# Head of batch 0 by feature halves, and new step plans, in a fused attention and token/channel mixing kernel

## The chip, the cores and the metric

One core of a Trainium2 chip. The metric is the device time of one execution in microseconds (us), the median of several runs. A ratio is the mean time of one kernel's runs over that of the other's runs in the same rounds, so it is not quite the ratio of the medians quoted beside it. Profiles cover one execution each; their span is about 1.8 us shorter than the time. The granted clock is the share of TensorE's full clock that the profile records as granted.

The engines: TensorE (PE, with its weight loads PEld), VectorE (DVE), ScalarE (ACT), GpSimd (POOL), SyncE (SP).

## The reference

Pooled attention with 8 batches, 8 heads, 576 tokens and head size 64, followed by a mixer: keys and values are averaged over groups of 8 tokens, so each head has 72 keys. The result is rearranged to x (576 tokens by 512 features) and goes through token mixing and channel mixing.

```python
k_p = k.reshape(B, H, 72, 8, D).mean(axis=3)            # and v_p
attn = softmax(q @ k_p.T / sqrt(D));  x = attn @ v_p     # -> (B, S, H*D)
h = np.maximum(xt @ w_tok1, 0.0) @ w_tok2                # token mixing, xt = x transposed
u = x + h.transpose(0, 2, 1)
out = u + np.maximum(u @ w_ch1, 0.0) @ w_ch2             # channel mixing, 512 -> 1536 -> 512
```

## The kernel before

Batch 0 has a *head* of its own: a list of steps that runs before any channel mixing can start. Then follow nine *units* (eight batches, and one for the 64 last tokens of all batches). A unit is 48 half-steps of channel mixing on PE: in the first 24 w_ch1 products (a group of four 512-column matmuls per two half-steps, ScalarE applies the relu), in the last 24 w_ch2 products. A *plan* says after which half-step which step of the attention of the next batches is put in: a bare name is for the next batch, `>` for the one after, `<` for the same one. The program gives each engine its instructions in the order in which the steps are put in, so a plan fixes the order on each engine.

```python
HEAD = """c0 c1 d8 q0 d1 q1 d5 kp0 kp1 kt0 d2 o0 e0 kt1 kp2 kp3 o1 e1 kt2 kt3 q2 q3 d2 o2 e2 vpool0 o3 d1 vpool1 e3 d2
          av1 av0 av2 d2 av3 at_0 at_2 av4 at_1 at_3 d2 at_4 X0 X1 X2 A0 A1 A2 X3 A3 d3"""
FIRST = {0: "<u0 lv2", 1: "<u1", 2: "<u2", 3: "<u3", 4: "k0 kpool1 lk3", 5: "Q0 Q1 Q2 Q3", 10: "kpT v0 v1 lq3 lv3",
         13: "s0", 17: "s1", 22: "s2", 24: "av0", ...}
FOURTH = {0: ">K0 >K1 >V0 >V1 at0", 1: "at1", 3: "u4 M4", 4: "u0", 6: "u1 M0", 7: "u2", 9: "u3 M2 M",
          15: ">Q0", 17: ">Q1", 18: ">kpT", 22: ">s0", 26: "T0", 27: ">Q2 >Q3 lq4 lk4 lv4", ... 32: ">s1", ...
          37: ">s2", 39: ">av0", 41: ">av1", 43: ">av2", 45: ">av3", 47: ">av4"}
```

(cut; SECOND, THIRD and LATER are alike.) The steps: `q`, `Q` q transposes by PE and by DVE; `k`, `v`, `kp`, `kpool`, `vpool`, `K`, `V` pooling; `kt`, `kpT` key transposes; `o`, `e`, `s` scores with exp on ScalarE; `av` attention times values, normalised by DVE; `at` first token product with relu; `u` second token product plus x, an add by DVE; `t` u transposed by PE; `M`, `T` the same by a round trip through memory and DVE block transposes; `X`, `A` the parts of u transposed directly in the head; `dN` N dummy matmuls that keep PE busy; `l` loads.

The pools hold eight PSUM banks (128 x 512 fp32 each): three accumulators of one bank (`p1`), two of two banks (`p2`), one more (`pt`).

```python
ps_one = ctx.enter_context(tc.tile_pool(name="ps_one", bufs=3, ...))   # p1
ps_two = ctx.enter_context(tc.tile_pool(name="ps_two", bufs=2, ...))   # p2
ps_tr  = ctx.enter_context(tc.tile_pool(name="ps_tr",  bufs=1, ...))   # pt
def u(c):                                   # cut: c < 4
    ps = ps_one.tile([P, 512], FP32, name="p1")
    for i, (w, a) in enumerate(mms):
        nc.tensor.matmul(out=ps, lhsT=w, rhs=a, start=(i == 0), stop=(i == len(mms) - 1))
    nc.vector.tensor_tensor(out=dst, in0=ps, in1=x, op=ALU.add)
```

The softmax here doesn't subtract the row's maximum and nothing guards it: scores larger than these inputs give would overflow.

## Time and profile before

| | before |
|---|---|
| time, median of the five runs beside the changed kernel | 280.1 us (279.3 to 280.5) |
| span of the profile | 278.3 us |
| PE busy | 268.9 us, 97% |
| first channel matmul | 24.75 us |
| last matmul ends | 274.5 us |
| waits of PE in the list, after 24.7 us | 1.3 us |

The 1.3 us are these five groups (what waited, for what, "issue" being nothing that the profile shows; us in total, times, longest). The prediction below shows the other lines and splits the time by them.

```profile
PE p L445 <- issue: 0.3, 2, 0.2
PE p L467 <- issue: 0.3, 2, 0.2
PE p L225 <- DMA kr<-in_k_dram: 0.3, 1, 0.3
PE p L297 <- ACT ex L263: 0.2, 1, 0.2
PE p L343 <- DVE xt L315: 0.2, 1, 0.2
```

### The profile page before, as it was taken

The page shows a single profiled execution, that of the slowest core. Times are in us where ns is not written, and L with a number is a line of the kernel's source. Part 1 is how long each engine was busy: PE and PEld are TensorE (multiplying, and loading weights), DVE is VectorE, ACT ScalarE, POOL GpSimd, SP SyncE. Part 2 cuts the span into 40 slices and gives each one's busy share as a digit, 9 for nine tenths or more (in the row PEclk, how much of TensorE's full clock was granted, in tenths as well). Part 3 has the DMA queues.
Part 4 walks back from the last instruction along what each step waited for, and adds up shares of the span by engine and source line. Part 5 has one row for each costly group of instructions (what it writes and reads, how often), then busy time and mean ns, then how long its engine had stood idle before and what let it go on. Part 6 is the DMA issues. An engine that isn't in the chain of part 4 may idle for free.

```text
span 278.3 us, 4495 instructions
## 1 busy us (share of the span) xinstructions
PE 268.9 (97%) x1790; PEld 130.9 (47%) x1824; DVE 141.8 (51%) x272; ACT 111.2 (40%) x187; POOL 130.8 (47%) x121
## 2 busy tenths in 40 slices
PE   8989999999999999999999999999999999999994
PEld 3755445444543545454445444544454444444443
DVE  5465967771575757275178545834584161011012
ACT  2543590039305533614741366046604602602600
POOL 8585222999996992898069999600000000000000
PEclk9999999999999999999999999999999999999999
DMA  7999999980299930793549562324132545015024
GB/s 162 185 203 206 205 203 187 225 179 10 24 180 180 231 50 0 138 218 89 115 74 241 144 129 49 77 66 126 38 78 57 136 71 115 0 39 113 2 44 108
DMA packets 36837, 32.68 MB, mean 117 GB/s; under 512 B 14288, under 2 KB 30288, under 8 KB 36816
## 3 DMA queue, kind: packets, MB, share of 16 engines
q0 software_dynamic: 18672, 17.64, 40.2%
q1 hardware_dynamic: 17984, 14.62, 20.9%
q8 instruction: 14, 0.23, 0.3%
q10 hardware_dynamic: 160, 0.13, 0.2%
q14 instruction: 7, 0.06, 0.1%
HBM read 38.21 MB, written 11.80 MB: 180 GB/s over the span
## 4 chain that ended last, share of the span: by engine, by line
PE 83%; DMA 8%; ACT 3%; DVE 2%; POOL 2%; issue 1%; POOLq 0%
PE p L467 32%; PE p L445 30%; PE p L358 6%; PE p L343 5%; DMA kr<-in_k_dram 5%; PE p L258 4%; PE p L297 3%; DMA f<-in_moe_w_tok_dram 3%; ACT ex L263 1%; PE pt L368 1%; PE p L479 1%; ACT GT L449 1%; DVE o L453 1%; POOL vr L86 1%; POOL kr L86 1%
## 5 line engine op out<-in xcount | busy, mean ns | idle before, releaser
L467 PE MATMUL p<-w_ch,GT 128*128 128x512 bf16 x404 | 99.2, 379 | 1.0 <-issue 0.3
L449 ACT ACTIVATE GT<-p 128x512 bf16<-128x512 f32 x108 | 64.0, 599 | 75.8 <-PE p L445 75.6
L445 PE MATMUL p<-uT,w_ch 128*128 128x512 bf16 x373 | 92.7, 379 | 1.1 <-issue 0.3
L445 PEld LDWEIGHTS <-w_ch 128*128 128x128 bf16 x432 | 40.3, 98 | 48.1 <-issue 4.9
L467 PEld LDWEIGHTS <-GT 128*128 128x128 bf16 x420 | 38.0, 98 | 41.9 <-issue 3.1
L453 DVE TENSOR_TENSOR o<-p,u 128x512 f32<-128x512 f32 x32 | 21.9, 684 | 31.4 <-PE p L467 31.2
L263 ACT ACTIVATE ex<-p 72x1024 bf16<-72x1024 f32 (+1 forms) x42 | 31.6, 807 | 10.8 <-PE p L258 10.8
L146 POOL TENSOR_TENSOR t<-t 72x512 f32<-72x512 f32 x24 | 30.3, 1262 | 1.9
L145 POOL TENSOR_TENSOR t<-kr 72x1024 f32<-72x1024 bf16 x12 | 25.5, 2123 | 8.5 <-DMA kr<-in_k_dram 7.8
L359 DVE TENSOR_TENSOR u<-p,x 128x512 bf16<-128x512 f32 x32 | 22.1, 691 | 13.9 <-PE p L358 13.6
L145 POOL TENSOR_TENSOR t<-vr 72x1024 f32<-72x1024 bf16 x12 | 25.4, 2120 | 0.9
L390 DVE STREAM_TRANSPOSE uT<-v 128x512 bf16<-128x512 bf16 x16 | 10.4, 686 | 23.7 <-DMA v<-mem 23.7
L334 ACT ACTIVATE AT<-p 128x512 bf16<-128x512 f32 x8 | 4.8, 597 | 42.0 <-PE p L343 39.2
L315 DVE TENSOR_TENSOR x<-p,den 128x512 bf16<-128x512 f32 x30 | 20.7, 691 | 1.0
L246 DVE STREAM_TRANSPOSE qD<-qb 128x576 bf16<-128x576 bf16 x28 | 20.5, 794 | 0.0
L297 PEld LDWEIGHTS <-ex 72*128 72x128 bf16 x320 | 15.3, 98 | 10.4 <-DVE x L315 0.8
L358 PE MATMUL p<-AT,w_tok 128*128 128x512 bf16 x63 | 18.8, 379 | 0.0
L297 PE MATMUL p<-vp,ex 72*128 72x65 bf16 x320 | 16.8, 194 | 1.0 <-DVE x L315 0.6
L309 DVE RECIPROCAL den<-p 128x8 f32<-128x8 f32 (+1 forms) x39 | 7.9, 203 | 17.5 <-PE p L297 16.6
L103 POOL DMA_DIRECT2D qb<-in_q_dram x7 | 5.1, 730 | 21.5 <-DVE qD L246 20.3
L343 PE MATMUL p<-x,w_tok 128*128 128x512 bf16 x54 | 14.1, 379 | 0.1
L336 DVE TENSOR_SCALAR AT<-p 128x512 bf16<-128x512 f32 x8 | 5.5, 692 | 13.4 <-PE p L343 12.6
(90 smaller groups left out, 206.4 us busy)
## 6 DMA issues: line engine op xcount, KB each, us to landing
out_dram<-o SPq DMA_DIRECT2D x70, 128.0 KB, 2.5
kr<-in_k_dram POOLq DMA_DIRECT2D x7, 576.0 KB, 11.8
qb<-in_q_dram POOLq DMA_DIRECT2D x7, 576.0 KB, 11.1
vr<-in_v_dram POOLq DMA_DIRECT2D x7, 576.0 KB, 15.2
w_ch<-in_moe_w_ch_dram POOLq DMA_DIRECT2D x6, 512.0 KB, 13.2
mem<-u SPq DMA_DIRECT2D x8, 256.0 KB, 2.1
v<-mem SPq DMA_DIRECT2D x8, 160.0 KB, 3.8
v<-mem SPq DMA_DIRECT2D x8, 128.0 KB, 3.0
```

The lines of the kernel that those rows point to most:

```text
L145: eng.tensor_tensor(out=t4[:, 0:n], in0=t[:, hs, 0:4], in1=t[:, hs, 4:8], op=ALU.add)
L146: eng.tensor_tensor(out=t4[:, 0:n, 0:2], in0=t4[:, 0:n, 0:2], in1=t4[:, 0:n, 2:4], op=ALU.add)
L263: nc.scalar.activation(out=exv[:, a, :, gs.start:gs.stop, n0:n0 + n], in_=pss[a][0:SP, :, 0:len(gs) * n].rearrange("j l (g n) -> j l g n", ...
L297: nc.tensor.matmul(out=halves[h // 4][:, (h % 4) * (D + 1):(h % 4 + 1) * (D + 1)], lhsT=st["ex"][:, h * S + n0:h * S + n0 + P], rhs=st["vp ...
L315: nc.vector.tensor_tensor(out=dst.rearrange("p (a h d) -> p a h d", a=2, d=D), in0=view[:, :, :, 0:D], in1=den[rows, :, :, None].broadcast ...
L343: nc.tensor.matmul(out=ps, lhsT=w_tok1[:, c if c < 4 else 4 + par, m * P:(m + 1) * P], rhs=st["x"][:, c, :] if c < 4 else st["xt"], start= ...
L358: nc.tensor.matmul(out=ps, lhsT=w, rhs=a, start=(i == 0), stop=(i == len(mms) - 1))
L359: nc.vector.tensor_tensor(out=dst, in0=ps, in1=x, op=ALU.add)
L445: nc.tensor.matmul(out=ps, lhsT=w_ch1[:, kk, m * P:(m + 1) * P], rhs=uT[:, kk, :], start=(kk == 0), stop=(kk == 3))
L449: nc.scalar.activation(out=GT[:, m, :], in_=ps, func=AF.Relu)
L453: nc.vector.tensor_tensor(out=o_sb, in0=ps, in1=(u_tails if n == B else st["u"])[:, c, :], op=ALU.add)
L467: nc.tensor.matmul(out=pss[c], lhsT=GT[:, m, c * P:(c + 1) * P], rhs=w_ch2[:, m, :], start=(m == 0), stop=(m == NM - 1))
```

## The change

Its intent: shorten the head, and place all steps with a model of the timeline. In the head, heads 4 to 7 are scored by token chunk instead of by pair; AV, normalising and token mixing are done per four heads, so that the first half can flow while the second is scored; u transposed is made in two passes; the later dummies are dropped. All plans are new, and the first unit takes the w_ch2 weights in fours (before: eight, then four).

```diff
+        def half_av(c, a, eng, bank):        # cut: four heads, one bank
+                for l in range(4):
+                    nc.tensor.matmul(out=ps[:, l * (D + 1):(l + 1) * (D + 1)], lhsT=st["ex"][...], rhs=st["vp"][:, h, :], ...)
+                nc.vector.reciprocal(out=den[rows], in_=view[:, :, D])
+                if eng == "D":  nc.vector.tensor_tensor(out=dst..., in0=view[:, :, 0:D], in1=den..., op=ALU.mult)
+                else:           # four scalar.activation(Copy, scale=den)
-        def at_tile(c):                      # two 512-column matmuls
+        def at_half(c, a, ms):               # 256 columns of one or both
+        def zscore(i):                       # heads 4 to 7, tokens of four, four and one blocks of 64
-            runs[0:2] = [(c, m, m + w) for m, w in ((0, 8), (8, 4)) for c in range(2)]
+            runs[0:2] = [(c, m, m + 4) for m in (0, 4, 8) for c in range(2)]
-    HEAD = (above)
+    HEAD = """c0 c1 d8 q0 d1 q1 d5 kp0 kp1 kt0 kp2 e0 o0 kt1 kp3 kt2 o1 q3 q2 e1 kt3 vpool0 z2 z0 w30A w10Dt
+              w00D z1 w20Dt vpool1 w40Dt g21 w11D w21Dp g20 g11 g40 g31 g10 w01D g30 g00 w31D h1 w41Dp g41 h0 h2
+              h3 g01 X1 h4 X2 Xa X3 Xb A0 A1"""
-    FIRST, SECOND, THIRD, FOURTH, LATER = (above)
+    FIRST = {0: "<u3 <u1", 1: "<u2 <u0", 2: "k0 lv2", 4: "Q0 Q1", 5: "lk3", 6: "lq3 Q3 Q2", 9: "v0", 10: "kpool1",
+             11: "lv3", 12: "kpT", 14: "s0", 15: "v1", 19: "s1", 25: "s2", 26: "av0", 27: "av1", 29: "av2", ...}
+    FOURTH = {0: "M4 u4 >K1", 1: "at0 at1 >K0", 3: "u0 >V0", 5: "u1 M0", 6: ">V1", 7: "u2", 8: "u3 M2", 9: "M",
+              15: ">kpT >Q1", 17: ">Q0", 22: "lq4", 25: ">Q2", 26: ">s0", 27: "T0", 28: ">Q3 lk4 lv4", ... 32: ">s1 T2", ...
+              39: ">av0", 41: ">av1", 42: ">av2", 45: ">av3", 46: ">av4"}
```

(cut: SECOND, THIRD, LATER, the other plan entries, the rewritten steps for u transposed, the registration of the step names, and two statements that are only written differently.)

## The prediction

> **What bounds the kernel now.** I read the page first, then busy time by stretch, then TensorE (PE) in order of time, because the change touches only the first 25 us and the order of steps after it.
>
> ```profile
> span 278.3 us, 4495 instructions
> PE 268.9 (97%) x1790; PEld 130.9 (47%) x1824; DVE 141.8 (51%) x272; ACT 111.2 (40%) x187; POOL 130.8 (47%) x121
> ...
> PE 83%; DMA 8%; ACT 3%; DVE 2%; POOL 2%; issue 1%; POOLq 0%
> ```
>
> PE is the bound. DVE, ACT and POOL are near half, so moving work onto them is free unless it lies in PE's way. The stretches tell where PE is not full:
>
> ```profile
> 0.00:5.00 5.00, 3.81 (x12) 1.56 (x13) 2.66 (x9) 1.96 (x2) 3.87 (x11) 1.00 0.63 158
> ...
> 24.70:52.00 27.30, 26.76 (x186) 12.71 (x188) 20.33 (x33) 12.36 (x22) 8.70 (x9) 1.00 1.26 198
> ...
> 246.00:274.50 28.50, 28.34 (x141) 13.88 (x142) 5.26 (x8) 7.17 (x12) 0.00 (x0) 1.00 0.28 62
> 274.50:278.30 3.80, 0.00 (x1) 0.00 (x0) 0.42 (x1) 0.00 (x0) 0.00 (x0) 1.00 0.42 98
> ```
>
> The second column is PE's busy time. From 24.7 to 274.5 us PE is busy nearly throughout, and the listed waits of PE after 24.7 us add up to 1.3 us, the longest 0.3. So time = (start of the first channel matmul) + (about 250 us of PE work) + 3.8 us of tail. The change does not touch the amount of work after the head. It can move the start, and it can remove or add small waits.
>
> ```profile
> 1.19 3.60 PE L513 MATMUL pt<-warm 128*128 128x512 bf16 x8 [1.19 <-DVE warm L535]
> ...
> 17.89 0.43 PE L297 MATMUL p<-vp,ex 72*128 72x65 bf16 x8 [0.55 <-DVE x L315]
> ...
> 20.96 0.59 PE L326 MATMUL p<-xt,w_tok 128*128 128x512 bf16 x2
> 21.39 0.83 PE L400 MATMUL p<-ident,x 128*128 128x128 bf16 x12
> 22.06 1.55 PE L408 MATMUL p<-w_tok,AT 128*128 128x512 bf16 x6
> 23.45 0.39 PE L400 MATMUL p<-ident,x 128*128 128x128 bf16 x4
> 23.89 0.38 PE L408 MATMUL p<-w_tok,AT 128*128 128x512 bf16 x1
> 24.10 0.81 PE L513 MATMUL pt<-warm 128*128 128x512 bf16 x3
> 24.75 0.59 PE L445 MATMUL p<-uT,w_ch 128*128 128x512 bf16 x2
> ```
>
> L513 are dummy matmuls. The head ends at 24.75 with three of them (24.10 to 24.75, 0.216 us each), right in front of the first channel matmul. Before that, the fourth mixing block is done late (23.45 and 23.89), after the other three.
>
> ```profile
> 17.74 0.17 DVE L303 RECIPROCAL den<-p 128x4 f32<-128x4 f32 x1
> 17.95 0.42 DVE L304 TENSOR_TENSOR x<-p,den 128x256 bf16<-128x256 f32 x1
> 18.29 0.17 DVE L303 RECIPROCAL den<-p 128x4 f32<-128x4 f32 x1
> 18.50 0.42 DVE L304 TENSOR_TENSOR x<-p,den 128x256 bf16<-128x256 f32 x1
> 18.84 0.20 DVE L309 RECIPROCAL den<-p 128x8 f32<-128x8 f32 x1
> ```
>
> VectorE sets the middle of the head: from 16.64 to 20.78 it normalises the AV results one after another. A half of a chunk (four heads) recurs every 0.55 us (17.74, 18.29, 18.84); a whole one takes 0.20 + 0.69 with small gaps, about 0.95. This is the price list for the change.
>
> **What the Trainium skill says.** "TensorE: Matmul & The Clock Gate", Back-to-back issue gap: N/2.4 + 2.5 ns, 216 ns at N = 512. The trace agrees (three dummies in 0.65 us). Same page, What's actually happening: the array runs at half rate until it has been busy for a window of about 3.4 us, and falls back after an idle one. The first eight dummies take 3.60 us, 0.45 each, so this trace shows the slow state once; the longest gap in the rest of the head is 0.55 us. "VectorE: DVE Perf Modes", The TRN2 errata: a fixed cost per instruction, so two halves cost more than a whole. The trace agrees: 0.42 us for 256 elements against 0.69 for 512.
>
> **The change part by part.**
>
> (a) Dummies. d8, d1, d5 stay; fourteen later ones go (2+2+1+2+2+2+3), 3.0 us of PE at 0.216. Most stood in waits and are worth nothing; the last three, 0.65 us, stood in front of the first channel matmul, though the last uT copy (ACT, 24.30 to 24.89) would have held part of that.
>
> (b) Heads 4 to 7 are scored by token chunk. Four exps (0.59 + 0.70 twice = 2.58 us of ACT) become two of 1024 columns and one of 256; in the first unit's score steps two exps of 72x1024 take 1.93 and two of 72x256 take 0.69, so 0.96 each and 0.35, together 2.3. ACT saves 0.3 us; the gain in order is that AV and mixing of heads 0 to 3 start before heads 4 to 7 are scored.
>
> (c) AV by halves. Ten halves: one by ACT (4 x 0.22 = 0.87), nine by DVE, 9 x 0.55 = 4.95 us. Before: DVE had four chunks, about 4.1 us. DVE gains 0.8 us of work, but may start some 2 us earlier.
>
> (d) Token mixing by halves: 20 matmuls of 256 columns instead of 10 of 512, the same 2.2 us of streaming. The last one before AT is now 2 x 0.11 instead of 2 x 0.22.
>
> (e) uT in two passes: all first-half products (4 x 0.216), then all second-half ones; the late fourth block disappears.
>
> My walk through the new head, with the landings and durations above. The loads are issued in the same order, so they land as before: the last v piece needed by the first value pooling is there at about 12.75 (the trace starts it at 12.95). Value pooling 12.75 to 13.8, its copy on DVE 13.8 to 14.25. z2, z0 on PE to 14.3; ACT exps z2 to 14.3, z0 to 15.3, first half chunk on ACT to 16.2, z1 to 17.1. DVE: reciprocal at 14.65, half chunks 14.85, 15.4, 15.95, then 0.2 us of waiting for the second value pooling, its copy 16.7 to 17.1, then six half chunks at 0.55: 17.1 + 3.3 = 20.4. (Before: 20.78.) Last mixing matmuls 20.5 to 20.85, relu ACT 20.8 to 21.4, DVE 20.9 to 21.6 (before 21.98 and 22.28). The 12 transposing matmuls left fit in the relu's shadow. A0 21.45 to 22.3, A1 22.3 to 23.2. Copies: DVE 22.7 to 23.4, ACT 22.95 to 23.55, DVE to 24.1, ACT to 24.1. The first channel matmul needs the first copy: **23.5 us instead of 24.75, 1.25 us earlier.**
>
> (f) First unit. Before, PE waited 0.27 us at 29.23 for the key load of batch 1, issued at 15.59 and 13.60 us on its way:
>
> ```profile
> 15.59 13.60 DMA kr<-in_k_dram
> 29.23 1.06 PE p L225 x8
> ```
>
> That pooling moves from step 4 to step 10. PE gets there at 23.5 + 8 x 0.216 (u) + 22 x 0.216 + waits of (g) = 30.4, after 29.2: 0.27 us gained. The key transpose follows at 32.1 (DVE's half, 29.2 + 2.4 = 31.6, is ready), the scores at 33.15, where the two q transposes end at 33.0. That is tight: it is the supply that would stop a still faster head.
>
> (g) The u products now come two by two in steps 0 and 2. There are three one-bank accumulators and each u needs a DVE add of 0.69 before its bank is free: by the same walk waits of 0.1, 0.25 and 0.08, 0.43 us, against 0.16 before. Lost: 0.27.
>
> (h) The other plans. What is left to gain is what PE still waits for after the first unit: 0.9 us in listed waits (four of 0.2 or so) and about seven of 0.08 on u accumulators, some 1.4 us. A plan placed by a model of the timeline may take part of it and may make new ones. I take 0.3 us.
>
> Sum: 1.25 + 0.27 - 0.27 + 0.3 = 1.55 us; 280.0 - 1.6 = **278.4 us**.
>
> **The rivals.**
> 1. *VectorE sets the head.* It has 0.8 us more to do. If the halves cannot start until about 16 us (the accumulators or the exps come late), its chain ends at 21.5 or later and the start stays at 24.7. Against: values are ready at 14.25 and DVE has nothing else then. It would make the time 279.8.
> 2. *The clock.* Without dummies PE is thinner between 10 and 21 us, and a fall to half rate would double the streaming time of what follows until the next busy window: some 3 us, time 281 to 283. Against: no wait in the walk reaches 1 us, and the measured ones with dummies were 0.55 at most.
> 3. *The transfers.* DMA is saturated until about 55 us (share 1.26 in the stretch above). The w_ch2 pieces land near 36.8, 39.9 and 43.0; PE needs the first at 40.4 before, about 38.8 after, and the new order in fours asks the second at 41.4 and the third at 44. Margin 1 to 2 us. If it failed, the head's gain would be given back there: 279.5 to 280.
> 4. *The plans make waits.* Reordering 200 steps may turn some 0.2 us waits into more; up to 1 us either way.
>
> **Range and chances.** Rivals 1 and 3 give back at most the gain; rival 2 is unlikely. The best I can sum (head 1.8, plans 1.2) is 277.0. So 278.4, with 277.0 to 280.1 eight times in ten. Two per cent is 5.6 us; PE's idle time before 25 us (25 less 22.7 busy, 2.3), the removed dummies (3.0) and the waits after it (1.3) together are hardly more, and most of the head hangs on transfers. Faster by over 2%: 0.02; within: 0.97; slower: 0.01.
>
> **What would show it.** Right: the first channel matmul at 23 to 24 us, no wait of PE on the key load, DVE half chunks every 0.55 us from about 14.8 to 20.4 in the order of PE, PE's end moved by the same 1 to 2 us. Wrong: the first half chunks on DVE after 16 us; PE gaps over 1 us in the head, or matmuls of 512 columns spaced 0.43 us; a wait on w_ch or on qD between 33 and 45 us; a list of PE waits after 60 us that sums to over 1.5 us.

## The result

275.5 us (274.9 to 276.0, five runs) against 280.1 in the same rounds: ratio 0.984, 95% interval 0.982 to 0.986. That is 4.6 us less, within 2% as predicted most likely, but outside the predicted range of 277.0 to 280.1.

The page of the changed kernel (span; busy time and instructions of each engine):

```profile
span 273.7 us, 4544 instructions
PE 266.1 (97%) x1832; PEld 130.4 (48%) x1832; DVE 141.9 (52%) x280; ACT 110.4 (40%) x182; POOL 131.1 (48%) x121
```

PE is the bound as before, and its share has not moved: 97%. A reader who looks only at this line sees nothing of where 4.6 us went. The order of time on PE, at the end of the head (start, duration, what):

```profile
21.28 1.92 PE L461 MATMUL p<-w_tok,AT 128*128 128x512 bf16 x8
23.34 0.59 PE L512 MATMUL p<-uT,w_ch 128*128 128x512 bf16 x2
...
30.22 1.04 PE L226 MATMUL p<-kr,ident 72*72 72x256 bf16 x8
```

The first channel matmul (L512) comes at 23.34, 1.41 us earlier than at 24.75; the walk had said 23.5. The key pooling at 30.22 has no wait any more (the walk: 30.4). PE's last matmul ends at 269.95 in the chain of the changed kernel and at 274.51 before. From first channel matmul to last that is 246.6 us against 249.8: **3.15 us less for exactly the same matmuls.** The predicted net gain for this part was 0.3 us.

So where were 3.15 us of waiting, if the list of PE's waits after 24.7 us added up to 1.3 in all (and to 0.4 in the changed kernel)? Two places of the kernel before, in order of time on PE:

```profile
128.86 0.59 PE L358 MATMUL p<-AT,w_tok 128*128 128x512 bf16 x2
129.38 0.81 PE L445 MATMUL p<-uT,w_ch 128*128 128x512 bf16 x3
...
150.86 0.81 PE L343 MATMUL p<-x,w_tok 128*128 128x512 bf16 x3
151.87 0.38 PE L343 MATMUL p<-xt,w_tok 128*128 128x512 bf16 x1 [0.20 <-DVE xt L315]
```

Look at the starts, not at the idle times. Two matmuls at 128.86 should let the next start 2 x 0.216 later, at 129.29; it starts at 129.38, 0.08 us late (a `u` accumulator whose add is not done), and no idle time is printed. Three at 150.86 should let the next start at 151.51; it starts at 151.87, 0.36 late, and 0.20 is printed. The record of a matmul of 512 columns lasts 0.379 us while matmuls follow each other every 0.216, so 0.163 us of every wait lies under the modelled end of the matmul before it. The Trainium skill says of these records ("Perfetto Trace Analysis", Per-instruction lifecycle) that TensorE's end is estimated, not observed; the trace puts the 0.163 on it. The same place in the changed kernel runs through, 4 x 0.216 from start to start:

```profile
146.93 1.03 PE L395 MATMUL p<-x,w_tok 128*128 128x512 bf16 x4
147.79 0.38 PE L395 MATMUL p<-xt,w_tok 128*128 128x512 bf16 x1
```

I then took, for every two neighbouring matmul records, the time from start to start less the streaming time of what the program has between them (N/2.4 + 2.3 ns at N columns, other small constants for the narrow ones; where a record is missing the next one is taken). The sums by unit, in us; the score steps have a fixed extra cost of about 0.36 a batch in it (three score steps, 0.12 each), the same in all kernels. Its level depends on the constants for the narrow matmuls; the differences between the kernels do not:

| kernel | first channel matmul | unit 0 | 1 | 2 | 3 | 4 | 5 | 6 | all |
|---|---|---|---|---|---|---|---|---|---|
| before | 24.75 | 1.56 | 2.41 | 1.02 | 0.73 | 0.89 | 0.53 | 0.18 | 7.4 |
| changed | 23.34 | 1.47 | 1.09 | 0.49 | 0.37 | 0.36 | 0.36 | 0.02 | 4.2 |

Take off 7 x 0.36 = 2.5 and 4.9 us could be had before, of which the list showed 1.3; 1.7 are left after. The gain is in units 1 to 6, which the old plans left 0.2 to 1.3 us a unit worse. For these six alone, the sums are 5.8 and 2.7 us, of which 6 x 0.36 = 2.2 are fixed: 3.6 us could be had, and the new plans took 3.1 of them. Units 7 and 8 have nothing beside them and no wait in either.

### The profile page after: what moved, and what is told of

Same layout as the page of the kernel before. It is cut to its first block, busy times and chain, and to the rows that moved or that the text cites. A ratio compares the mean times of both kernels' runs of the same rounds, so it can differ in the third digit from the quotient of the medians.

```text
span 273.7 us, 4544 instructions
## 1 busy us (share of the span) xinstructions
PE 266.1 (97%) x1832; PEld 130.4 (48%) x1832; DVE 141.9 (52%) x280; ACT 110.4 (40%) x182; POOL 131.1 (48%) x121
## 4 chain that ended last, share of the span: by engine, by line
PE 89%; DMA 3%; ACT 3%; DVE 2%; POOL 1%; issue 1%; POOLq 0%
PE p L534 33%; PE p L512 32%; PE p L410 6%; PE p L395 6%; PE p L344 3%; PE p L260 3%; DMA vr<-in_v_dram 3%; ACT ex L265 1%; PE pt L420 1%; ACT GT L516 1%; PE p L226 1%; PE p L546 1%; POOL kr L86 1%; PE pt L376 1%; PE p L461 0%
## 5 line engine op out<-in xcount | busy, mean ns | idle before, releaser
L534 PE MATMUL p<-w_ch,GT 128*128 128x512 bf16 x420 | 101.5, 379 | 0.0
L512 PE MATMUL p<-uT,w_ch 128*128 128x512 bf16 x384 | 92.8, 379 | 0.1
L512 PEld LDWEIGHTS <-w_ch 128*128 128x128 bf16 x432 | 40.6, 98 | 47.3 <-issue 2.5
L147 POOL TENSOR_TENSOR t<-t 72x512 f32<-72x512 f32 x24 | 30.4, 1265 | 1.9
L362 DVE TENSOR_TENSOR x<-p,den 128x512 bf16<-128x512 f32 x28 | 19.4, 692 | 1.0
L386 ACT ACTIVATE AT<-p 128x512 bf16<-128x512 f32 x7 | 4.2, 597 | 32.2 <-PE p L395 32.2
L344 PEld LDWEIGHTS <-ex 72*128 72x128 bf16 x280 | 13.0, 98 | 7.9 <-DVE x L362 0.7
L356 DVE RECIPROCAL den<-p 128x8 f32<-128x8 f32 (+1 forms) x35 | 7.1, 202 | 15.9 <-PE p L344 15.4
L344 PE MATMUL p<-vp,ex 72*128 72x65 bf16 x280 | 14.1, 193 | 0.2 <-ACT ex L265 0.2
L260 PE MATMUL p<-qD,kD 32*72 32x512 bf16 (+1 forms) x224 | 11.4, 294 | 0.1
```

The lines of the kernel that those rows point to most:

```text
L147: eng.tensor_tensor(out=t4[:, 0:n, 0:2], in0=t4[:, 0:n, 0:2], in1=t4[:, 0:n, 2:4], op=ALU.add)
L344: nc.tensor.matmul(out=halves[h // 4][:, (h % 4) * (D + 1):(h % 4 + 1) * (D + 1)], lhsT=st["ex"][:, h * S + n0:h * S + n0 + P], rhs=st["vp ...
L512: nc.tensor.matmul(out=ps, lhsT=w_ch1[:, kk, m * P:(m + 1) * P], rhs=uT[:, kk, :], start=(kk == 0), stop=(kk == 3))
L534: nc.tensor.matmul(out=pss[c], lhsT=GT[:, m, c * P:(c + 1) * P], rhs=w_ch2[:, m, :], start=(m == 0), stop=(m == NM - 1))
```

## The experiments

Theory P: the surprise is many short waits of PE that the plans removed. Theory H: the earlier head carries the rest along. Rivals of detail came up on the way.

**1. The new head with the old plans.** The changed kernel with `FIRST` to `LATER` and the order in eights put back.

> The new head with the old step plans and the old order in eights. Theory P (the plans carry the surprise): the first channel matmul comes at 23.3 us as in the changed kernel, but the old first plan has the key pooling of batch 1 at step 4; PE gets there near 27.6 and stands until the keys land near 29.1, a wait of about 1.5 us that takes the head's 1.4 us back. So 279.7 to 280.2 us. Theory H (the head carries it, the rest follows from an earlier start): 277 us or less.

Measured 280.89 us against 280.21 (ratio 1.002, 0.9996 to 1.0036): the head alone gains nothing. The start was at 23.38 as expected. Its longest listed waits after 24 us:

```profile
PE p L260 <- DVE qD L248: 1.0, 2, 0.7
PE p L226 <- DMA kr<-in_k_dram: 0.5, 1, 0.5
```

The wait on the keys (L226) was only 0.64 us from start to start (0.5 listed), since the keys landed near 28.4; that part of the expectation was too large. The u accumulators took 0.5. The rest went in unit 3, where the scores (L260) stood for the q transposes, and these stood on DVE behind the first block transpose, which waited for the round trip through memory: one store of u took 4.3 us to land instead of 2.1. Unit 3's sum was 1.99 instead of 0.73. So the total came near the expected one (0.7 above its range), but in part by two further waits that I had not foreseen.

**2. The new plans with the old head.** The kernel before with `FIRST` to `LATER` and the order in fours of the changed one.

> The old head with the new step plans and the order in fours. Theory P: first channel matmul at 24.75 as before, then the 3.1 us of small waits are gone, 276.8 to 277.4 us. Theory H: 279.5 us or more.

Measured 277.14 us (ratio 0.988, 0.986 to 0.990): theory P. In its trace the sum of small waits is 3.9. Its first channel matmul came at 25.38; seven profiled runs with the old head and its dummies spread from 24.75 to 25.67, so the profile of before was at the early end. This kernel and the changed one differ by the head alone: 277.14 and 275.5 us, 1.6 apart by the medians and some 1.2 by the two ratios (0.988 and 0.984).

**3. Only the plans of the second and later units.**

```diff
-    SECOND, THIRD, FOURTH, LATER = (old)
+    SECOND, THIRD, FOURTH, LATER = (new)      # FIRST, HEAD and the order in eights stay
```

> The kernel before with only the plans of the second and later units replaced. By start-to-start times of TensorE the first unit holds about 1.2 us of small waits in both kernels, so under theory P nearly all of the 3.1 us comes here: 276.9 to 277.6 us. If the new first plan carried it: 279 us or more.

Measured 277.41 us (ratio 0.9895, 0.988 to 0.991). Nearly all of the plans' gain is here, 0.3 us at most in the first unit.

**4. The complement: the changed kernel with the old later plans.**

```diff
-    SECOND, THIRD, FOURTH, LATER = (new)
+    SECOND, THIRD, FOURTH, LATER = (old)      # new HEAD, new FIRST
```

> The changed kernel with only the plans of the second and later units put back to the old ones. Theory P with the sums of small waits by unit: the old later plans hold 3.1 us more than the new ones, so 275.5 + 3.1 = 278.6 us, up to 279.9 if unit 3 meets the wait on the q transposes that the head-only run met (1.3 us). Theory H (the early start carries the rest with it): 276.5 or less.

Measured 279.97 us median (ratio 0.9985, 0.995 to 1.002), in two groups: 278.6, 278.9, 279.1 and 280.8, 280.9, 280.9. The lower group is at the expected 278.6, though not for the expected reasons alone: the profiled run, the one of 278.62 us, had 1.51 in unit 3 already (0.8 more than before), and its channel started at 22.85, 0.5 earlier than in the changed kernel's profile. What makes the upper group 2 us slower was not seen in a trace and stays open; the granted clock of two of its runs was 0.991 and 0.994, of the third 0.999. Theory H (276.5) falls.

**5. Three kinds of short waits taken out by hand.** The kernel before with three sets of moves: S for score steps, U for u products, X for the last AV chunks, which write the tail of x.

```diff
-  FIRST  ... 17: "s1", 22: "s2", 24: "av0"      +  18: "s1", 23: "s2", 25: "av0"       # S; alike in SECOND and THIRD
-  LATER  ... 4: "u0", 6: "u1 M0", 7: "u2", 9: "u3 M2 M"
+             5: "u0", 7: "u1 M0", 9: "u2", 11: "u3 M2 M"                                # U; FOURTH alike
-  FOURTH ... 43: ">av2", 45: ">av3", 47: ">av4" +  42: ">av2", 44: ">av3", 46: ">av4"  # X; in THIRD av3 and av4 alone
```

> The kernel before with three kinds of waits taken out by hand, none of which the list of waits shows in full: the second score step one step later in the first three units (0.27 us four times, the exps not done), the u products of the later units two steps apart (0.08 us eight times, the add not done), the fifth AV chunk one step earlier in the third and fourth unit (0.21 and 0.36 us, the tail of x not ready). Theory P in detail: 2.2 us together, 277.6 to 278.2 us. If these short waits were not real, or only moved, 279.5 us or more.

Measured 279.62 us (ratio 0.9966): 0.9 us instead of 2.2. In the trace the waits of U and X were gone (0.64 and 0.57 less). Those of S were gone at `s1` and partly back at `s2` (0.23 or 0.25, three times) and at an AV step (0.37, twice). In unit 3, where `M` now starts two half-steps later, some 0.5 came up in front of the scores, on the q transposes that stand behind the first block transpose. The next three runs take these apart.

**6. S alone.**

> The kernel before with only the second score step (and the third and the first AV with it) one step later in the first three units. From the run of all three edits: the four waits of 0.27 us go, but 0.23 us comes back at the third score step three times and 0.37 at the first AV twice, since ScalarE has 6.5 us of exps and relus to do in that stretch. So no gain: 279.7 to 280.3 us. If the distance of the steps were all: 279.0 us.

Measured 280.09 us (ratio 0.9992, 0.998 to 1.0005): no gain, as expected. ScalarE in the kernel before, in order of time:

```profile
61.49 1.93 ACT L263 ACTIVATE ex<-p 72x1024 bf16<-72x1024 f32 x2 [0.39 <-PE p L258]
63.31 1.07 ACT L449 ACTIVATE GT<-p 128x512 bf16<-128x512 f32 x2
64.26 1.94 ACT L263 ACTIVATE ex<-p 72x1024 bf16<-72x1024 f32 x2
66.07 1.58 ACT L449 ACTIVATE GT<-p 128x512 bf16<-128x512 f32 x3
67.50 0.69 ACT L263 ACTIVATE ex<-p 72x256 bf16<-72x256 f32 x2
```

From 61.49 to 68.19 it has no pause: exps (L263) and the channel relus (L449) share it. An engine that is busy 40% of the span is the bound for these 6.7 us, and a step moved by one half-step only changes which matmul waits for it.

**7. U and X with a well-meant third move.** The q transposes of unit 3 put before the first block transpose:

```diff
-  FOURTH ... 26: "T0", 27: ">Q2 >Q3 lq4 lk4 lv4"
+             25: ">Q2 >Q3", 26: "T0", 27: "lq4 lk4 lv4"     # and U with "u0 u1 M0" at 5, and X
```

> The kernel before with two of the three hand edits, the ones whose waits vanished in the run of all three: the u products of the later units where no accumulator is short (0.08 us eight times), the fifth AV chunk earlier (0.21 and 0.36), and in unit 3 the q transposes put before the first block transpose on VectorE, so that they cannot stand behind a transfer. The score steps stay. Theory P: 1.1 to 1.3 us less, 278.9 to 279.2 us. If short waits only move: 279.8 us or more.

Measured 283.13 us median, 280.7 to 288.5 (ratio 1.006): slower. Two of the six runs, 287.4 us and the profiled one, 288.5, count as slow by being over 1.5% above its fastest; the four fast ones (280.7 to 283.5) are slower than the kernel before too, but none of them was traced. The trace of the slow one shows a collision. DVE, then the transfers issued between 133 and 137 us (count, KB each, us to landing):

```profile
150.08 0.71 DVE L390 STREAM_TRANSPOSE uT<-v 128x512 bf16<-128x512 bf16 x1 [16.21 <-DMA v<-mem]
```

```profile
qb<-in_q_dram POOLq DMA_DIRECT2D x1, 576.0 KB, 5.7
kr<-in_k_dram POOLq DMA_DIRECT2D x1, 576.0 KB, 10.1
vr<-in_v_dram POOLq DMA_DIRECT2D x1, 576.0 KB, 14.3
v<-mem SPq DMA_DIRECT2D x4, 128.0 KB, 10.2
```

The q buffer came free 7 us earlier, so the loads of the next batch were issued at 134.2 us instead of 141.6, on top of the four reads of the round trip (v<-mem). Those landed up to 150 us instead of 139, DVE stood 16 us for them, PE stood twice (5.0 and 2.6 us), and the granted clock was 0.50 from 148.5 to 158.7 us.

**8. The same without that move.**

> The run with the u and AV edits again, but with the q transposes of unit 3 left behind the first block transpose as in the kernel before. In the earlier run the q buffer came free 7 us sooner, the next batch's loads were issued at 134 instead of 141 us and took the bandwidth from the round trip of u through memory (landed at 150 instead of 139). Theory L (that collision alone made it slow): this one is 1.0 to 1.3 us under the kernel before, 278.9 to 279.2, with the loads issued near 141 us. If the u and AV edits themselves cause it: 282 us or more again.

Measured 278.85 us (278.6 to 279.1, ratio 0.995, 0.994 to 0.996): 1.3 us less, theory L, and every run is below the fastest one with the third move. The reads of the round trip:

```profile
v<-mem SPq DMA_DIRECT2D x4, 128.0 KB, 3.5
```

They land in 3.5 us again. Twelve moved entries of the plans, and waits of which not one is listed above 0.2 us, are worth 1.3 us.

**9. The plans-only kernel without the fourteen later dummies.** This tests the rival of the clock.

> The kernel of the plans-only run without the fourteen later dummy matmuls of the old head. If the dummies cost only where they stand before ready work: the channel matmuls start 0.4 to 0.8 us earlier, 276.3 to 276.8 us. If the clock needs them, 512-column matmuls in the head are spaced 0.43 us and the time is 278 us or more. What is then left to the changed kernel's 275.5 is what the halves bring, 0.8 to 1.2 us.

Measured 277.27 us (276.2 to 277.7, ratio 0.988, 0.986 to 0.991) against 277.14 with the dummies in the earlier rounds: no gain, and between my two expectations. The stretches of the head in its trace (PE's busy time second, the granted clock third from the end), and two rows of PE:

```profile
18.00:20.00 2.00, 1.40 (x11) 0.57 (x12) 1.90 (x7) 1.35 (x7) 1.94 (x5) 0.78 1.25 206
20.00:22.00 2.00, 2.00 (x13) 1.03 (x12) 1.26 (x3) 0.00 (x0) 2.00 (x3) 0.50 1.24 206
```

```profile
18.88 1.83 PE L326 MATMUL p<-x,w_tok 128*128 128x512 bf16 x4
...
25.75 0.59 PE L445 MATMUL p<-uT,w_ch 128*128 128x512 bf16 x2
```

The clock falls to half; four token matmuls (L326) take 1.83 us, where four in the head of before took 1.03 (at 19.66). The channel starts at 25.75, not earlier than with dummies. The executions agree: five of the six had a mean granted clock of 0.992 or 0.993 and took 276.9 to 277.7 us, the sixth had 0.998 and took 276.2, while none of the four with dummies was under 0.998. So in the old head the dummies hold the clock, and dropping them gave back what it saved; the 276.2 is a single run without a trace. The changed head does without them: in both traces of the unedited kernel the granted clock is 1.00 from where its record begins (4.5 and 4.9 us) to the end.

**10. An attempt at a better version.** The changed kernel with the remaining waits of its first two units moved:

```diff
-  FIRST  = {0: "<u3 <u1", 1: "<u2 <u0", 2: "k0 lv2", 4: "Q0 Q1", ... 14: "s0", 19: "s1", 25: "s2", 26: "av0", 27: "av1"
+  FIRST  = {0: "<u3", 2: "lv2", 3: "<u1", 5: "<u2 lk3", 6: "lq3", 7: "<u0", 8: "k0 Q0 Q1 Q3 Q2", ... 15: "s0 v1", 20: "s1", 25: "s2", 27: "av0", 28: "av1"
-  SECOND ... 3: "s0 lk3 >V0", 8: "s1", 13: "s2"   +  3: "lk3 >V0", 4: "s0 >K0", 9: "s1", 14: "s2"
```

> The changed kernel with five small waits of its first two units taken out by moving steps: u3, u1, u2, u0 one at a time (0.42 us), the first score step of both units one step later (0.19 and 0.36), AV one step after the last exp (0.3). Theory P: 1.0 to 1.3 us less than the changed kernel, 274.2 to 274.6 us. If the waits come back elsewhere (the exps of ScalarE are the limit between the score steps): 275.2 us or more.

Measured 275.26 us (ratio 0.983): the second line of the expectation, the waits came back elsewhere. Of the 1.27 us that were to go, 0.24 were not waits at all but the fixed 0.12 of the two score steps, which no move removes. To compare with the changed kernel on one chip, both ran again:

> The changed kernel once more, beside the next one. 275.3 to 275.8 us; both theories.

> The version with five waits moved, beside the changed kernel on the same chip. Its waits sum to 0.24 us less in the trace: 275.0 to 275.5 us, the two not to be told apart. If the edits are worth what the waits were: 274.4 us.

Measured 275.31 us for the changed kernel (ratio 0.983, 0.981 to 0.985) and 275.53 for the attempt (ratio 0.983, 0.982 to 0.985): the two cannot be told apart, as the sums in the traces (4.1 and 4.0) say. The waits of the u products and the first scores went; others came at the key transpose (0.22), at three AV steps and at the third score step of unit 1 (0.26). The profiled run of the attempt, 278.33 us (fast by the 1.5% rule, but 2.8 above the median), caught something else. Its PE waits, and its stretches:

```profile
PE p L376 <- DMA w_tok<-in_moe_w_tok_dram: 1.6, 1, 1.6
```

```profile
16.00:18.00 2.00, 0.40 (x6) 0.26 (x6) 0.92 (x3) 0.56 (x1) 2.00 (x2) 0.76 1.23 201
18.00:20.00 2.00, 2.00 (x20) 1.61 (x19) 1.13 (x5) 0.00 (x0) 1.94 (x5) 0.50 1.24 206
```

A piece of w_tok landed at 17.7 us instead of 16.1 (it was issued at the same time), PE stood 1.6 us in front of the first token product (L376), the clock fell to half until 23.8 us, and the first channel matmul came at 26.42 instead of 23.04. The head of this attempt is the changed kernel's head, so the changed kernel has that risk too. Of the other outliers, the one of 277.6 us in the first six runs of the attempt may be this (its granted clock was 0.991; the profiled one's 0.987), but was not profiled; the changed kernel's one at 276.3 had 0.999, which does not fit.

## Why the prediction was wrong

- **Head, parts (a) to (e): right.** Start of the channel 23.34 us in the trace, 23.5 predicted; the head's worth under the new plans 1.2 to 1.6 us (experiment 2), 1.25 predicted. That the two profiles lie only 1.41 us apart is partly luck, since old heads started at 24.75 to 25.67 and new ones at 22.85 to 23.38 (without the late transfer of experiment 10); DVE half chunks every 0.55 us from 14.9 to 20.25 (predicted 14.85 to 20.4). That the dummies are worth nothing in the waits was wrong for the old head (experiment 9: the clock falls without them), but not for the new one.
- **First unit, parts (f) and (g): right.** Key pooling at 30.22 without a wait (30.4); first scores at 33.05 (33.15), where 0.19 us showed, 0.12 of them the fixed cost of a score step, so 0.07 of waiting for the q transpose; the u products waited 0.42 us (0.43). Unit 0 is a draw, 1.56 against 1.47.
- **The other plans, part (h): this is the step that failed.** The prediction put "What is left to gain" at "some 1.4 us" and took 0.3. The measured gain of the later units is 3.1 us by the traces, 2.8 us by experiment 3. The mechanism named (plans remove small waits) was right, the size was wrong by ten, and two factors made it so. The ceiling was read from the list of waits, which leaves out 0.163 us of every wait behind a 512-column matmul: start to start, what could be had after the first unit was 3.6 us, not 1.4. And the share that the plans would take was guessed at a fifth (0.3 of 1.4); they took 3.1 of 3.6. Neither alone accounts for the result: a fifth of 3.6 is 0.8, and all of 1.4 would have given 277.4 us (both worked out from the numbers above). With 3.1 in place of 0.3 the prediction's sum is 1.25 + 0.27 - 0.27 + 3.1 = 4.35, so 275.7 us.
- The best case was set by the same reading: "The best I can sum (head 1.8, plans 1.2) is 277.0".
- **Rival 1** (VectorE sets the head) did not come. **Rival 2** (the clock) was dismissed because "no wait in the walk reaches 1 us"; it is real, and that test is not the right one. The clock fell in the old head without dummies, where the longest wait before it was 0.8 us, and in the new head when one transfer was late (1.6 us); it did not fall in experiment 6, where PE stood 1.5 us for the keys (6.5 to 8.1 us). **Rival 3** (transfers) did not come in the changed kernel: no wait on w_ch is listed. It did come in unit 3 of three variants (experiments 1, 4 and 7), at a place that I had not looked at. **Rival 4** gave "up to 1 us either way"; it was the main term.
- The parts do not add: head alone 0, plans alone 3.1, both 4.6 to 4.8. The head needs the plans, which put the key pooling and the q transposes where an earlier PE does not meet late transfers (experiments 1 and 4).

Open: why one store of u takes 4.0 to 4.3 us in experiments 1 and 4 instead of 2.1, and the slower half of the executions of experiment 4.

## What to carry to other kernels

Where PE is at 97%, judge the waits by the starts of neighbouring matmuls against their streaming time, and not by idle time: short waits sit under the modelled ends, and here they summed to several times the listed ones. Before moving a step, look at what else its engine does in that stretch and which buffer it frees: an earlier free buffer starts a load earlier, and that load may hit a transfer that something waits for. An earlier start is worth only what the next late transfer leaves of it, and dummy matmuls that look idle may be holding the clock.

## What the Trainium skill lacked or had wrong

- "Perfetto Trace Analysis", Per-instruction lifecycle, says that TensorE's end time is estimated, but not what follows for finding waits: a 512-column record lasts 0.379 us at a spacing of 0.216, so behind such a matmul waits up to 0.163 us show no idle time and longer ones are short by that much. Here 4.9 us of avoidable waits were listed as 1.3.
- "TensorE: Matmul & The Clock Gate", HAM oscillation, gives the rule of no idle gaps over about 3.4 us; the heading after it names frequent short idle between matmul groups as a second way to a fall, without a figure. Here the granted clock fell to 0.50 in the head without a gap of 3.4 us: the longest listed waits in the 5 us before it were 0.8 us (experiment 9) and 1.6 us (experiment 10), in stretches of 2 us of which PE's records covered 1.40 and 0.40 us. How thin is too thin cannot be read off: PE was busy 0.54 of 2 us in experiment 6 (6 to 8 us) and 1.33 in experiment 2 (18 to 20 us) at a granted clock of 1.00. By the clock records of the traces, the stretches at half lasted 3.41 us (experiment 9), 6.83 (10) and 10.24 (7).
- No page has the chain from a freed SBUF buffer through an earlier load to a slowed round trip through memory: the reads went from 3.5 us to 10.2 us each (median) when 1.7 MB of loads were issued 7 us earlier.
